# A second normalisation moved to the head of the next step in ScalarE's order, two more q tiles ahead of the attention chain, and transposed reloads spread between W_down's loads

## The chip, the cores and the metric

The kernel runs on one core of a Trainium2 chip. The metric is device microseconds of one execution. Each time below is the median of a few executions; most agree within 0.3%. The profile is one execution taken by the hardware profiler. Its span is some 2 us shorter than the time of the same execution (849.7 against 851.4 us before).

## The reference, cut to what matters

```python
# A_x: 1 x 2048 x 1024, bf16; 32 heads of 32; F = 3584
x = A_x
h  = x + attention(layernorm(x)) @ wo          # linear attention: phi(q) kv / (phi(q) z)
h2 = h + (relu(g) * u) @ W_down                # g, u = layernorm(h) @ W_gate, @ W_up
# phi(t) = where(t > 0, t + 1, exp(t)) + 1e-6
```

The kernel works on tiles of 128 tokens, 16 in all.

## The kernel before: the parts that matter

Five engines (TensorE, VectorE, ScalarE, GpSimd, and SyncE, which issues the DMAs) run their own instruction lists, each in program order, and meet through semaphores. A helper adds every operation to the list of one engine and works out the waits, so **program order in the source is the order in each engine's queue**.

The attention chain has 16 steps (`t`). `a1` makes one q tile: 8 matmuls on TensorE into a bank (a slice of its output memory), then `exp` on ScalarE, then two VectorE operations (together "phi"). `a2(t)` multiplies phi(q) by kv ("num") and divides on VectorE. `a4(t-2)` is the output projection, then the residual `h`, its statistics, and the second normalisation ("norm2"). The time from one num to the next is called the pitch.

```python
def phi(b, w, dst_ap, dst_buf, name):            # end of every a1
    PL.add("act", exp(out=Et, in_=bank(b)))      # L533
    PL.add("dve", tensor_scalar(out=E2t, Et, min 1.0, add 1e-6))          # L535
    PL.add("dve", scalar_tensor_tensor(out=dst_ap, bank(b), E2t))         # L538
# ...
def a4(st):
    # 16 matmuls into a pair of banks
    PL.add("dve", tensor_tensor(out=hsb[:, hs, :], ps pair + x2))         # L698, "h"
    dma(h_scr <- hsb)
    ks = ln_stats(hsb[:, hs, :], ...)    # dve: bn_stats x2 (L509), aggr, ve (L514); pool: rstd (L517)
    PL.add("pool", nmr = -mean * rstd)                                    # L706
    PL.add("act", xn = Identity(hsb * rstd + nmr))                        # L710, "norm2"
    # DMA of xn: transposed into hnT (tiles 0-7), or to hn_scr in DRAM (tiles 8-15)
# ...
for ct in range(NG):
    a1(0, ct)                            # q tiles of the first 512 tokens
rest = [(r, ct) for r in range(1, NSB) for ct in range(NG)]     # 24 more
LAG = 2
for t in range(NST):
    a2(t)                                # "num t"; num 4, 8, 12 need q tiles of the next 512 tokens
    if rest: a1(*rest.pop(0))            # q tile a
    if t >= LAG: a4(t - LAG)
    if rest: a1(*rest.pop(0))            # q tile b
    if t == 13: s_sums()                 # "S sums": four VectorE sums for the product stage
    if t == 14: [f_() for f_ in t_sums(0) + t_sums(1)]          # "T sums": eight more
for t in range(NST - LAG, NST):
    a4(t)
```

After the chain come two passes, each a product stage (gate and up, by Strassen products P1, P7, P6, ...) and four W_down rounds. The start of P6, the third product of the first pair, is used below as the mark of the chain's end. W_down streams through a ring of four chunks. Before the second pass eight tiles of norm2's output are reloaded with transposition.

```python
for i, (hf, dh) in enumerate(rounds):            # four W_down rounds of a pass
    if p_ + 1 < NPASS and i == 0:
        for t in range(TPP):                     # eight transposed reloads, in one burst
            dma_t(sl_ht[t], hnT[...], hn_scr[...], reads=[B_hnscr[t]], writes=[B_hnT[t]])
    d_round(p_, hf, dh, ...)                     # per chunk of W_down: 16 matmuls, then load_wd_next()
    if p_ + 1 < NPASS and i == 1:
        s_sums()
```

## Time and profile before

| what | before |
|---|---|
| time, median | 852.99 us (852.23 to 853.74) |
| span in the profile, granted TensorE clock | 849.7 us, 0.972 |
| TensorE busy | 791.0 us, 93% |
| num 0 to the first P6 product | 142.2 to 308.1 us |
| TensorE's wait in the first W_down round | 6.9 us |

From the profile page of the kernel before: the span, then busy tenths in 40 slices of 21 us for TensorE and VectorE and the granted clock, then the chain that ended last.

```profile
span 849.7 us, 9959 instructions
...
PE   8999999878685689999999969999999999999998
...
DVE  7455427746566966676667210315666766521111
...
PEclk9999999989897899999999989999999999999999
...
PE 81%; DVE 9%; issue 4%; SPq 2%; ACT 1%; POOL 1%; DMA 1%; DVEq 0%; ACTq 0%; POOLq 0%
```

TensorE has holes in two places: slices 8 to 15 (the attention chain), and slice 24 (the first W_down round). The clock falls in five of them (9, 11, 13, 14 and 24).

From the waits of the kernel before (engine, line, who was waited for: us in total, times, longest):

```profile
DVE RX L535 <- ACT RX L533: 90.1, 43, 10.9
PE ps L499 <- DVE RAB L538: 24.2, 7, 6.7
PE ps L499 <- DVE RO L674: 11.7, 11, 5.6
PE ps L499 <- DMA RW<-in_B_W_down_dram: 6.9, 1, 6.9
```

VectorE waits for `exp` (L533), and TensorE waits for phi (L538, before a num). Neither says yet why `exp` is late. The timeline does: TensorE, VectorE and ScalarE in one full step of the kernel before (start, duration, what; in brackets the idle time before and what ended it).

```profile
181.61 1.89 PE L499 MATMUL ps<-RAB,RC 128*128 128x512 bf16 x8
...
185.06 0.15 DVE L514 TENSOR_SCALAR ve<-mv 128x1 f32<-128x1 f32 x1
...
186.33 1.24 ACT L710 ACTIVATE xn<-hsb,nmr,rstd 128x1024 bf16<-128x1024 bf16 x1 [7.39 <-POOL nmr L706]
187.47 1.06 ACT L533 ACTIVATE RX<-ps 128x512 bf16<-128x512 f32 x2
...
188.08 0.29 DVE L535 TENSOR_SCALAR RX<-RX 128x512 bf16<-128x512 bf16 x1 [2.87 <-ACT RX L533]
```

The matmuls of q tile b (the first line) are done at 183.5 us, and ScalarE is idle. But norm2 stands ahead of their `exp` in ScalarE's queue. It needs the statistics that VectorE ends at 185.2 us and GpSimd's two small operations, so it starts at 186.3 and `exp` at 187.5. VectorE meanwhile idles 2.87 us: it waits for ScalarE, which waits for GpSimd, which waited for VectorE.

The first W_down round in the timeline of the kernel before, TensorE and SyncE's queue of DMA issues:

```profile
475.49 13.98 PE L499 MATMUL ps<-RW,RAB 128*128 128x512 bf16 x63
...
476.17 12.21 SPq L436 DMA_TRANSPOSE hnT<-hn_scr  x8
488.56 1.87 SPq L432 DMA_DIRECT2D RX<-h_scr  x4
490.53 2.73 SPq L432 DMA_DIRECT2D RW<-in_B_W_down_dram  x4
496.39 3.88 PE L499 MATMUL ps<-RW,RAB 128*128 128x512 bf16 x11 [6.93 <-DMA RW<-in_B_W_down_dram]
```

TensorE works through the four chunks in the ring in 14 us. The slot of the first was free at about 479, but the load that refills it is issued at 490.5, behind eight reloads and four loads of h.

### The profile page before, as it was taken

To read this page: it belongs to the slowest core of one execution; us is meant where nothing else is said; L and a number is where in the kernel's file an instruction comes from. 1 tells how busy PE (TensorE), PEld (TensorE's weight loads), DVE (VectorE), ACT (ScalarE), POOL (GpSimd) and SP (SyncE) were. 2 spreads that over 40 slices of the span, in tenths; PEclk is the share of its full clock that TensorE was granted. 3 is DMA by queue.
4 is the path that set the end of the run, shared out by engine and by line. 5 is a ranking of instruction groups with operands and counts; after the bars stand their busy time and mean duration, and the time that the engine had idled before them with its cause. 6 is when DMAs were issued, how large, how long until landed. Compare 5 with 4: busy or idle time off the path is not lost.

```text
span 849.7 us, 9959 instructions
## 1 busy us (share of the span) xinstructions
PE 791.0 (93%) x3719; PEld 362.6 (43%) x3791; DVE 433.2 (51%) x900; ACT 245.8 (29%) x402; POOL 25.2 (3%) x60
## 2 busy tenths in 40 slices
PE   8999999878685689999999969999999999999998
PEld 3444444433332234444444424444444444444443
DVE  7455427746566966676667210315666766521111
ACT  4333333122221145444554100003454445410000
POOL 2000000000000110000000000000000000000000
PEclk9999999989897899999999989999999999999999
DMA  8687200334334453331333665653233224026652
GB/s 297 174 203 194 61 2 11 78 87 100 91 108 88 121 176 100 99 94 57 99 100 95 141 202 191 211 201 117 81 100 100 75 75 123 1 75 200 206 189 98
DMA packets 160128, 102.37 MB, mean 120 GB/s; under 512 B 50384, under 2 KB 153040, under 8 KB 160080
## 3 DMA queue, kind: packets, MB, share of 16 engines
q1 hardware_dynamic: 160080, 101.73, 41.0%
q8 instruction: 30, 0.49, 0.2%
q14 instruction: 18, 0.15, 0.1%
HBM read 79.69 MB, written 10.49 MB: 106 GB/s over the span
## 4 chain that ended last, share of the span: by engine, by line
PE 81%; DVE 9%; issue 4%; SPq 2%; ACT 1%; POOL 1%; DMA 1%; DVEq 0%; ACTq 0%; POOLq 0%
PE ps L499 81%; DVE st L509 2%; DVE hsb L698 2%; DVE RO L674 1%; SPq L436 1%; ACT RX L533 1%; DVE RAB L538 1%; DVE RX L535 1%; DMA RW<-in_B_W_down_dram 1%; POOL rstd L517 1%; DVE rden L667 0%; DVE RC L728 0%; DVE dtmp L663 0%; DVE mv L512 0%; DMA RO<-RO 0%
## 5 line engine op out<-in xcount | busy, mean ns | idle before, releaser
L499 PE MATMUL ps<-RW,RAB 128*128 128x512 bf16 x878 | 194.3, 381 | 7.9 <-DMA RW<-in_B_W_down_dram 6.9
L499 PE MATMUL ps<-RC,RE 128*128 128x512 f16 x672 | 156.0, 382 | 2.8 <-ACT ps L755 2.8
L499 PEld LDWEIGHTS ps<-RW,RAB 128*128 128x128 bf16 x896 | 87.9, 98 | 113.9 <-DMA RW<-in_B_W_down_dram 7.4
L499 PE MATMUL ps<-RAB 128*128 128x512 bf16 x499 | 112.4, 379 | 1.6 <-ACT RAB L571 0.7
L755 ACT ACTIVATE ps<-ps 128x512 f32<-128x512 f32 x112 | 65.1, 582 | 161.2 <-PE ps L499 160.6
L861 DVE TENSOR_TENSOR RX<-ps,RX 128x512 bf16<-128x512 f32 x32 | 22.1, 692 | 174.4 <-PE ps L499 153.8
L499 PE MATMUL ps<-hnT,wring 128*128 128x512 bf16 x448 | 105.8, 379 | 0.0
L499 PEld LDWEIGHTS ps<-RC,RE 128*128 128x128 f16 x672 | 66.0, 98 | 83.3 <-ACT ps L755 3.3
L755 ACT ACTIVATE RO<-ps 128x512 f32<-128x512 f32 x112 | 66.7, 597 | 53.9 <-PE ps L499 53.9
L805 DVE TENSOR_TENSOR RAB<-ps,RAB 128x512 bf16<-128x512 f32 x28 | 19.4, 692 | 112.6 <-PE ps L499 112.6
L499 PEld LDWEIGHTS ps<-RAB 128*128 128x128 bf16 x512 | 49.3, 98 | 57.9 <-ACT RAB L571 0.9
L499 PEld LDWEIGHTS ps<-hnT,wring 128*128 128x128 bf16 x448 | 43.9, 98 | 53.1 <-issue 0.5
L499 PE MATMUL ps<-RW,RO 128*128 128x512 bf16 x249 | 62.4, 403 | 2.7 <-DMA RO<-RO 2.1
L535 DVE TENSOR_SCALAR RX<-RX 128x512 bf16<-128x512 bf16 x64 | 18.6, 291 | 90.3 <-ACT RX L533 90.1
L499 PE MATMUL ps<-RAB,RC 128*128 128x512 bf16 x250 | 64.2, 407 | 0.4
L533 ACT ACTIVATE RX<-ps 128x512 bf16<-128x512 f32 x64 | 37.2, 592 | 70.6 <-PE ps L499 45.8
L499 PE MATMUL ps<-RC,wring 128*128 128x512 f16 x224 | 52.9, 379 | 0.0
L710 ACT ACTIVATE xn<-hsb,nmr,rstd 128x1024 bf16<-128x1024 bf16 x16 | 19.8, 1240 | 114.1 <-POOL nmr L706 114.1
L755 ACT ACTIVATE RAB<-ps 128x512 bf16<-128x512 f32 x56 | 33.4, 597 | 62.0 <-PE ps L499 62.0
L499 PE MATMUL ps<-hnT,RE 128*128 128x512 bf16 x196 | 46.9, 379 | 1.5
L499 PE MATMUL ps<-kvz,RAB 128*128 128x132 bf16 x128 | 14.2, 230 | 36.6 <-DVE RAB L538 24.2
L744 DVE TENSOR_TENSOR RE<-wring,RE 128x512 f16<-128x512 bf16 x112 | 47.2, 421 | 1.9
(56 smaller groups left out, 537.5 us busy)
## 6 DMA issues: line engine op xcount, KB each, us to landing
RW<-in_B_W_down_dram SPq DMA_DIRECT2D x56, 512.0 KB, 3.5
wring<-in_B_W_gate_dram SPq DMA_DIRECT2D x28, 512.0 KB, 3.7
wring<-in_B_W_up_dram SPq DMA_DIRECT2D x28, 512.0 KB, 4.8
RAB<-in_A_wqkv_dram SPq DMA_DIRECT2D x8, 512.0 KB, 8.4
RX<-in_A_x_dram SPq DMA_DIRECT2D x16, 256.0 KB, 3.1
h_scr<-hsb SPq DMA_DIRECT2D x16, 256.0 KB, 3.2
RX<-h_scr SPq DMA_DIRECT2D x32, 128.0 KB, 3.6
out_dram<-RX SPq DMA_DIRECT2D x32, 128.0 KB, 1.7
```

Source lines behind the costliest of these rows:

```text
L436: return PL.add("sp", lambda e: e.dma_start_transpose(dst_ap, src_ap), reads=reads, writes=writes, slot=slot, name=name)
L499: lambda e: e.matmul(out_ap, lhsT, rhs, start=start, stop=stop, skip_group_check=skip),
L509: PL.add("dve", lambda e, c=c: e.bn_stats(out=st6[:, k, c * 6:(c + 1) * 6], in_=src_full[:, c * BCH:(c + 1) * BCH]), reads=[src_chunk_bufs ...
L517: PL.add("pool", lambda e: e.tensor_tensor(out=rstd[:, k, :], in0=ve[:, k, :], in1=neghalf[:], op=ALU.pow), reads=[B_ve[k], B_neghalf], wr ...
L533: PL.add("act", lambda e: e.activation(out=Et[:, k, 0:w], in_=src, func=ACTF.Exp), reads=[B_bank[b]], writes=[B_E[k]], name=name + "_exp")
L535: PL.add("dve", lambda e: e.tensor_scalar(out=E2t[:, k, 0:w], in0=Et[:, k, 0:w], scalar1=1.0, scalar2=1e-6, op0=ALU.min, op1=ALU.add), rea ...
L698: PL.add("dve", lambda e: e.tensor_tensor(out=hsb[:, hs, :], in0=ps[:, b:b + 2, :], in1=x2[:, xs, :].rearrange("p (a c) -> p a c", a=2), o ...
L710: PL.add("act", lambda e: e.activation(out=xn[:, kx, :], in_=hsb[:, hs, :], func=ACTF.Identity, bias=nmr[:, ks, :], scale=rstd[:, ks, :]), ...
L744: PL.add("dve", lambda e: e.tensor_tensor(out=Tring[:, k, j], in0=in0, in1=in1, op=ALU.subtract), reads=reads, writes=[B_T[k][j]], name="T ...
L755: PL.add("act", lambda e: e.activation(out=dst, in_=src, func=func), reads=reads, writes=writes, name=name)
L805: PL.add("dve", lambda e: e.tensor_tensor(out=hh[:, f1, 0:SBW], in0=bank(BA[1]), in1=r11[:, rr, :], op=ALU.mult), reads=[B_bank[BA[1]], B_ ...
L861: PL.add("dve", lambda e: e.tensor_tensor(out=outst[:, k, :], in0=bank(banks4[j], NW), in1=hres[:, k, :], op=ALU.add), reads=[B_bank[banks ...
```

## The change

Three parts. No arithmetic is added or removed.

1. Norm2 of tile t-3 moves to the head of step t, so that in ScalarE's order it no longer stands between `exp` a and `exp` b of the step that makes its input. In ScalarE's own list that is one place later, behind `exp` b, because `a2` puts nothing on ScalarE. (The T sums move from step 14 to 15.)
2. Two q tiles are made ahead of the loop, so that num 4, 8 and 12 find their last q tile a whole step old.
3. The eight reloads are spread: one after each of the first four W_down loads of rounds 0 and 1. (The second pass's S sums, which read what is reloaded, move from behind round 1 into round 2.)

```diff
+            a4_k[st] = ks
+
+        a4_k = {}
+
+        def a4_norm(st):            # norm2 and the DMA of its output, unchanged
+            hs = st % NHS
+            ks = a4_k[st]
             kx = st % NXN
@@ d_round, after each chunk
                 load_wd_next()
-                for _ in range(2):
-                    if fill:
-                        fill.pop(0)()
+                if fill:
+                    fill.pop(0)()
@@ the chain
         rest = [(r, ct) for r in range(1, NSB) for ct in range(NG)]
+        for _ in range(2):
+            a1(*rest.pop(0))
         LAG = 2
-        fill = []
-        for t in range(NST):
-            a2(t)
+        for t in range(NST + LAG + 1):
+            if t >= LAG + 1:
+                a4_norm(t - LAG - 1)
+            if t < NST:
+                a2(t)
             if rest:
                 a1(*rest.pop(0))
-            if t >= LAG:
+            if LAG <= t < NST + LAG:
                 a4(t - LAG)
 ...
-            if t == 14:
+            if t == 15:
                 for f_ in t_sums(0) + t_sums(1):
                     f_()
-        for t in range(NST - LAG, NST):
-            a4(t)
@@ the W_down rounds
-                if p_ + 1 < NPASS and i == 0:
-                    for t in range(TPP):
-                        dma_t(... "T5s_%d" % t ...)
-                d_round(p_, hf, dh, ...)
-                if p_ + 1 < NPASS and i == 1:
-                    s_sums()
+                late = []
+                if p_ + 1 < NPASS and i < 2:
+                    for t in range(i * STB, (i + 1) * STB):
+                        late.append(lambda t=t: dma_t(... "T5s_%d" % t ...))
+                if p_ + 1 < NPASS and i == 2:
+                    late.append(s_sums)
+                d_round(p_, hf, dh, ..., fill=late)
```

More of the change, by code (lines that the diff above doesn't have):

```diff
@@ L984, in bass_sequential_preLN__linear_attn_block__glu_gated_reglu__prompt_kernel @@
             for i, (hf, dh) in enumerate(rounds):
-                if p_ + 1 < NPASS and i == 0:
-                    for t in range(TPP):
-                        dma_t(sl_ht[t], hnT[:, :, t * P:(t + 1) * P], hn_scr[t * P:(t + 1) * P, :],
-                              "T5s_%d" % t, reads=[B_hnscr[t]], writes=[B_hnT[t]])
-                d_round(p_, hf, dh, [0, 1, 2, 3] if i % 2 == 0 else [4, 5, 6, 7])
-                if p_ + 1 < NPASS and i == 1:
-                    s_sums()
+                late = []
+                if p_ + 1 < NPASS and i < 2:
+                    for t in range(i * STB, (i + 1) * STB):
+                        late.append(lambda t=t: dma_t(
+                            sl_ht[t], hnT[:, :, t * P:(t + 1) * P], hn_scr[t * P:(t + 1) * P, :],
+                            "T5s_%d" % t, reads=[B_hnscr[t]], writes=[B_hnT[t]]))
+                if p_ + 1 < NPASS and i == 2:
+                    late.append(s_sums)
+                d_round(p_, hf, dh, [0, 1, 2, 3] if i % 2 == 0 else [4, 5, 6, 7], fill=late)
+                assert not late
         PL.finalize(eng_sems)
```

## The prediction

> **What bounds the kernel now.** The chain of waits is 81% TensorE. By the busy table by stage, two stretches have holes: the attention chain, from the first num tile at 142 us to the first P6 product at 308.1 us (about 42 us idle, granted clock 0.89 and 0.85), and the start of the first W_down round, 475.8 to 502 us (7 us idle, clock 0.87).
>
> *Chain.* By the timeline a full step needs on TensorE 0.48 (num) + 1.73 (q tile) + 3.45 (output projection) + 1.73 (q tile) = 7.4 us, on VectorE 2.4 (divide) + 0.94 (phi) + 2.96 (h and statistics) + 0.94 (phi) = 7.2 us. But the ten steps from num 2 (151.6) to num 12 (264.7) take 11.3 us each. The cause is ScalarE's order: exp a, norm2, exp b. Norm2 waits for VectorE's statistics and GpSimd (2.9 us from their end to VectorE's next phi), and exp b, whose matmul is done, waits behind it: VectorE idles 2.9 us, released by ScalarE, in each step. Num 4, 8 and 12 consume the last q tile at once, so TensorE waits 6.5 to 6.7 us there, then runs slow: 8 matmuls take 3.6 us instead of 1.9. The Trainium skill ("TensorE: Matmul & The Clock Gate", Part 1) states half rate after idling; 0.43 us apart against 0.22, these agree.
>
> *W_down.* Eight transposed reloads hold SyncE's queue from 476.2 to 488.4, so the fifth W_down chunk, its slot free at 479, is issued at 490.5. TensorE waits 6.9 us, then 20 matmuls take 5.8 us instead of 4.4: 8.3 us together.
>
> **The change** adds and removes no arithmetic.
> 1. Norm2 of tile t-3 heads step t in ScalarE's order. Between its statistics (step t-1) and phi a VectorE has phi b and the divide, 3.3 us, against the 2.9 us path: exp b no longer waits, exp a hardly.
> 2. Two q tiles (3.5 us TensorE) move ahead, so num 4, 8 and 12 find theirs a step old. The 1.4 us wait before num 0 goes.
> 3. Each reload follows one W_down load. A chunk lasts 3.45 us on TensorE; by the DMA shares, load plus reload need about 3 us. The stall should go.
>
> **Sum.** Num 0 moves to 145.7 us. Steps 0 and 1 (no projection) take 8.3 us; nine steps at 7.45 end at 221. VectorE, 2.4 us behind, bounds the tail: five divides 12, seven h 20.7, S and T sums 8.3, idle 1 to 2, so its last statistics end near 266.5, and P6 starts 3.1 us later, as now: 269.6 against 308.1. Saving 38.5 us. W_down: of 8.3 us I expect 8. 853.0 - 38.5 - 8.0 = 806.5; the interlock will not be perfect: **807 us**, range 800 to 817. Faster by over 2%: 0.97; within 2%: 0.025; slower: 0.005.
>
> **What would show it.** Step 1: VectorE's wait on exp (90 us in all) falls by over 25 us, step pitch 7.4 to 7.8 us. Step 2: TensorE's wait on phi (24.2 us) nearly vanishes. Step 3: no TensorE wait on W_down, and round one is 8 us shorter. VectorE bounds the tail; the 2.8 us wait before P6 stays or grows.
>
> **What would make it wrong.** If the 0.4 us slack before exp a is missing, norm2 moves its wait to exp a: pitch 8 to 9 us, 812 to 820 in total. If reloads slow W_down loads beyond 3.45 us each, part of the 8 us stays.

## The result, and the profile after

The time after is **802.23 us** (802.01 to 802.45, 2 runs) against 852.99 us; ratio 0.9405, 95% interval 0.9365 to 0.9445.

The same lines of the profile page, after:

```profile
span 800.3 us, 9969 instructions
...
PE   8999999999987799999999999999999999999998
...
DVE  7455535799999656756755103137657657401111
...
PEclk9999999999998999999999999999999999999999
...
PE 91%; DVE 5%; issue 1%; DMA 1%; ACT 1%; SPq 0%; POOL 0%; DVEq 0%; POOLq 0%; ACTq 0%
```

The holes of slices 8 to 11 and of the W_down round are gone. What is left is in slices 12 to 14, the tail of the chain. In slices 9 to 11 VectorE and TensorE are both at 90% or more.

The waits after. The line of TensorE waiting for phi (L538) and the one of TensorE waiting for W_down are not in the list any more. L762 is ScalarE's copy of a bank in the product stage. (Norm2's line is now L717.)

```profile
DVE RX L535 <- ACT RX L533: 58.6, 32, 10.9
...
PE ps L499 <- DVE RO L674: 7.4, 6, 5.5
...
PE ps L499 <- ACT ps L762: 4.8, 1, 4.8
```

A full step after (timeline of TensorE, VectorE and ScalarE):

```profile
181.63 1.89 PE L499 MATMUL ps<-RAB,RC 128*128 128x512 bf16 x8
...
183.61 0.60 ACT L533 ACTIVATE RX<-ps 128x512 bf16<-128x512 f32 x1 [3.28 <-PE ps L499]
...
184.71 0.15 DVE L514 TENSOR_SCALAR ve<-mv 128x1 f32<-128x1 f32 x1
184.78 0.28 DVE L535 TENSOR_SCALAR RX<-RX 128x512 bf16<-128x512 bf16 x1
...
185.97 1.24 ACT L717 ACTIVATE xn<-hsb,nmr,rstd 128x1024 bf16<-128x1024 bf16 x1 [1.76 <-DVE dtmp L663]
...
187.12 0.57 ACT L533 ACTIVATE RX<-ps 128x512 bf16<-128x512 f32 x1
...
188.09 0.28 DVE L535 TENSOR_SCALAR RX<-RX 128x512 bf16<-128x512 bf16 x1
```

`exp` b starts as soon as its matmuls are done, and VectorE goes from the statistics to phi b with no gap, where it lost 2.87 us before. Norm2 still has to wait for its input, which GpSimd ends at 185.85 us, and `exp` a (187.12) still stands behind it, 1.4 us after its own matmuls. But VectorE has the divide to do first and takes up phi a at 188.09, 0.4 us after that `exp` has ended: the wait has moved to where nobody is kept by it. From num 2 (153.61 us) to num 11 (220.22) a step takes 7.40 us. The first P6 product starts at 267.1 us instead of 308.1: 41.0 us of the 49.4 by which the span fell. The other 8.4 us come after it.

The first W_down round after (timeline of TensorE and SyncE's queue):

```profile
434.55 29.73 PE L499 MATMUL ps<-RW,RAB 128*128 128x512 bf16 x134
...
438.25 0.38 SPq L432 DMA_DIRECT2D RW<-in_B_W_down_dram  x1
438.68 1.45 SPq L436 DMA_TRANSPOSE hnT<-hn_scr  x1
441.70 0.39 SPq L432 DMA_DIRECT2D RW<-in_B_W_down_dram  x1
442.13 1.24 SPq L436 DMA_TRANSPOSE hnT<-hn_scr  x1
```

Each refill now goes out 3.5 us after the one before, as its slot comes free, and TensorE runs through without a wait.

### The profile page after: what moved, and what is told of

Its sections match the earlier page's. It is cut to its first block, busy times and chain, and to the rows that moved or that the text cites. A ratio compares the mean times of both kernels' runs of the same rounds, so it can differ in the third digit from the quotient of the medians.

```text
span 800.3 us, 9969 instructions
## 1 busy us (share of the span) xinstructions
PE 777.7 (97%) x3719; PEld 360.3 (45%) x3791; DVE 432.3 (54%) x900; ACT 246.8 (31%) x402; POOL 25.2 (3%) x60
## 4 chain that ended last, share of the span: by engine, by line
PE 91%; DVE 5%; issue 1%; DMA 1%; ACT 1%; SPq 0%; POOL 0%; DVEq 0%; POOLq 0%; ACTq 0%
PE ps L499 91%; DVE st L509 1%; DVE hsb L698 1%; DVE RO L674 1%; DMA RAB<-in_A_wqkv_dram 1%; ACT RX L533 1%; DVE RAB L538 1%; DVE RC L735 0%; DVE RX L535 0%; DVE RE L751 0%; DVE rden L667 0%; DVE dtmp L663 0%; SPq L432 0%; DVE mv L512 0%; PE ps L568 0%
## 5 line engine op out<-in xcount | busy, mean ns | idle before, releaser
L762 ACT ACTIVATE ps<-ps 128x512 f32<-128x512 f32 x112 | 65.1, 582 | 152.9 <-PE ps L499 149.1
L762 ACT ACTIVATE RO<-ps 128x512 f32<-128x512 f32 x112 | 66.7, 597 | 53.7 <-PE ps L499 53.7
L499 PE MATMUL ps<-RW,RO 128*128 128x512 bf16 x249 | 59.1, 388 | 0.4
L499 PE MATMUL ps<-RAB,RC 128*128 128x512 bf16 x250 | 58.0, 379 | 0.3
L762 ACT ACTIVATE RAB<-ps 128x512 bf16<-128x512 f32 x56 | 33.4, 597 | 62.2 <-PE ps L499 62.2
L535 DVE TENSOR_SCALAR RX<-RX 128x512 bf16<-128x512 bf16 x64 | 18.4, 288 | 58.6 <-ACT RX L533 58.6
L751 DVE TENSOR_TENSOR RE<-wring 128x512 f16<-128x512 bf16 x112 | 42.0, 416 | 0.0
L819 DVE TENSOR_TENSOR RO<-ps,RO 128x512 f32<-128x512 f32 x56 | 38.7, 691 | 5.5 <-ACT RO L762 5.4
```

Source lines behind the costliest of these rows:

```text
L499: lambda e: e.matmul(out_ap, lhsT, rhs, start=start, stop=stop, skip_group_check=skip),
L535: PL.add("dve", lambda e: e.tensor_scalar(out=E2t[:, k, 0:w], in0=Et[:, k, 0:w], scalar1=1.0, scalar2=1e-6, op0=ALU.min, op1=ALU.add), rea ...
L751: PL.add("dve", lambda e: e.tensor_tensor(out=Tring[:, k, j], in0=in0, in1=in1, op=ALU.subtract), reads=reads, writes=[B_T[k][j]], name="T ...
L762: PL.add("act", lambda e: e.activation(out=dst, in_=src, func=func), reads=reads, writes=writes, name=name)
L819: PL.add("dve", lambda e, w=w: e.tensor_tensor(out=ftmp[:, 4 + w, :], in0=bank(BF_[w]), in1=ftmp[:, 2 + w, :], op=ALU.add), reads=[B_bank[ ...
```

## The experiments

Twelve kernels, all correct, each timed against the kernel before in three rounds on the same chip. "Before" was 851.09, 851.52 and 850.66 us in the three groups. The first four runs of the table were on one chip and the other eight on another, so differences of under 1 us between groups say nothing. P6 is the start of the first P6 product in the profile, that is, the end of the chain.

| run | time, us | ratio to before | P6 at, us |
|---|---|---|---|
| norm_only | 818.03 | 0.9611 | 274.0 |
| q_only | 834.78 | 0.9813 | 292.6 |
| reload_only | 841.26 | 0.9889 | 307.9 |
| norm_and_q | 810.16 | 0.9520 | 267.5 |
| norm_mid | 802.13 | 0.9423 | 267.5 |
| half_bursts | 805.51 | 0.9467 | 268.0 |
| q_one | 801.41 | 0.9419 | 266.5 |
| q_six | 833.81 | 0.9798 | 289.7 |
| t_early | 798.29 | 0.9384 | 264.8 |
| s_late | 799.06 | 0.9392 | 263.3 |
| norms_late | 795.20 | 0.9346 | 262.5 |
| tail | 790.05 | 0.9285 | 256.9 |

By the record's rule for 2%, q_only and q_six are "unclear" and reload_only is "same". Their 95% intervals (0.9794 to 0.9831, 0.9779 to 0.9818, 0.9870 to 0.9908) all stay below 1: these gains are real, but near or under 2%.

### The parts one at a time

**norm_only**: the change without its second and third part.

```diff
-        for _ in range(2):            # against the changed kernel
-            a1(*rest.pop(0))
   and the reloads in one burst, as in the kernel before
```

> Only the second normalisation moves (no extra q tiles, reloads in one burst as before). Theory: it removes the 2.9 us that VectorE loses in every step, so the pitch falls from 10.1 to about 7.4 us, but num 4, 8 and 12 still consume a q tile made one step earlier. VectorE runs 2.4 us behind, its phi b ends about 9.65 us after its step began, so TensorE should wait about 2 to 2.5 us at num 4, 8 and 12 (6.7 us before). Time about 818 us (815 to 823), W_down stall unchanged at about 7 us. Rival: the stall at every fourth num is the true cause and the normalisation only a follower; then the waits at num 4, 8 and 12 stay near 6 us and the time stays above 830.

Measured: 818.03 us (816.87 to 819.15). TensorE's waits, norm_only:

```profile
PE ps L499 <- DVE RAB L538: 7.5, 4, 2.2
```

The four waits are 1.4 us at num 0 and 1.9, 2.0 and 2.2 us at num 4, 8 and 12 (2 to 2.5 were expected), where there were 6.5 to 6.7 us. The rival falls: most of the stall at every fourth num was itself made by norm2 in ScalarE's queue.

**q_only**: the kernel before with the second part alone.

```diff
         rest = [(r, ct) for r in range(1, NSB) for ct in range(NG)]
+        for _ in range(2):
+            a1(*rest.pop(0))
```

> Only the two extra q tiles ahead (norm2 between the two exps as before). Theory: waits on phi at num 4, 8, 12 vanish (24 us of waits before), but VectorE still loses 2.9 us per step to exp b behind norm2, pitch 10.1 us throughout, so num 12 comes near 250 us instead of 264.7; time about 836 us (833 to 841). Rival: the slack of one step hides norm2's wait as well, pitch near 7.4 us, time near 811. Second rival: neither part alone helps, time above 845.

Measured: 834.78 us. TensorE no longer waits for phi, but for the divide (L674):

```profile
PE ps L499 <- DVE RO L674: 19.7, 19, 5.6
```

Num 5 to num 11 follow each other in 10.1 to 10.2 us (177.97 to 239.01 us in the trace for six steps). The slack of a step doesn't hide norm2's wait. Nor does more of it:

**q_six**: the same with six tiles ahead.

```diff
+        for _ in range(6):
+            a1(*rest.pop(0))
```

> The kernel before with six q tiles ahead instead of none (norm2 in its old place, reloads in one burst). Theory: with norm2 in its old place VectorE loses 2.9 us in every step that has a q tile after norm2, however far ahead the tiles are; each pair moved ahead costs 3.5 us in front and turns one step of 10.1 us into one of 5.35 us, 1.3 us gained per pair: 834.8 - 2.6 = 832 us (830 to 834). Rival: more slack hides norm2's wait, the pitch falls towards 7.4 us, time below 820.

Measured: 833.81 us (832.38 to 835.45), within the expected range, its median 1.8 us above the 832 worked out; P6 comes 2.9 us sooner than in q_only, but the wait for W_down was 7.6 us in this profile and 6.2 in that of q_only. The pitch from num 5 to num 10 is 10.1 to 10.2 us again. The wait is a loop through three engines' queues, and work done ahead of a loop does not shorten it.

**q_one**: the changed kernel with one tile ahead instead of two.

```diff
-        for _ in range(2):
+        for _ in range(1):
             a1(*rest.pop(0))
```

> The changed kernel with one q tile ahead instead of two. Theory: with one tile ahead the last tile that num 4, 8 or 12 needs is the first q tile of the step before, whose phi ends 5.8 us after that step began, before the num at 7.4 us: no wait, so the second tile buys nothing; 801.5 us (800.5 to 803). Rival: two are needed, waits of 1 us or more at each fourth num, 804 to 806 us.

Measured: 801.41 us, and no wait for phi. One tile is enough; the second buys nothing that these runs can see.

**reload_only** and **norm_and_q**: the third part alone, and everything but it.

```diff
   reload_only = the kernel before, with the "late" list of the change in the W_down rounds
   norm_and_q  = the changed kernel, with the burst of eight reloads of the kernel before
```

> Only the reloads spread, one after each of the first four W_down loads of rounds 0 and 1. Theory: the stall of 6.9 us and the slow matmuls after it vanish, nothing else moves: 844.6 us (843.5 to 845.5). Rival: what the reloads cost is DMA time, not the place in the queue, so W_down loads now come late by a little in several chunks: TensorE waits on W_down stay at 3 us or more, time above 847.

> Everything but the spread of the reloads. Theory: the parts at different places in the program add up: 802.2 + 8.4 = 810.6 us (809.5 to 812), with the W_down stall back at 6.9 us and the chain as in the changed kernel (first P6 product at 267 us). Rival: the spread also changed the chain or the chain's earlier end changes the stall: off by 2 us or more.

Measured: 841.26 and 810.16 us. In reload_only the wait on W_down is gone. Its gain of 9.8 us is above the expected 8.4, so 841.26 us misses the expected range on the fast side. In the two profiles 8.4 us are gained from the start of the first W_down round on. The rest lies at P6, long before a reload is issued: the first eight P6 matmuls took 1.90 us here and 3.50 in the profile of the kernel before, after the same wait of 2.77 us. The clock came out differently. (No trace shows P6 in the other executions.) This is the line in the timeline of the kernel before:

```profile
308.12 3.50 PE L499 MATMUL ps<-RC,RE 128*128 128x512 f16 x8 [2.77 <-ACT ps L755]
```

and in that of reload_only:

```profile
307.86 1.90 PE L499 MATMUL ps<-RC,RE 128*128 128x512 f16 x8 [2.77 <-ACT ps L755]
```

The gains of the three runs (33.1, 16.3 and 9.8 us) add up to 59.2, and the whole change gained 50.8. Norm2 and the q tiles overlap: together 40.9 us, not 49.4, because both take from the stall at every fourth num. After norm_only the q tiles are worth 7.9 us, about its 7.5 us of waits for phi. The reloads stand apart: norm_and_q less the changed kernel (timed in other rounds) is 7.9 us. The wait for W_down in the profile of norm_and_q was 5.4 us, not the 6.9 that were expected.

### Is it norm2's place, or the age of its input?

**norm_mid**: norm2 goes back between the two exps, but for the tile one step older.

```diff
-            if t >= LAG + 1:
-                a4_norm(t - LAG - 1)
             if t < NST:
                 a2(t)
             if rest:
                 a1(*rest.pop(0))
+            if t >= LAG + 1:
+                a4_norm(t - LAG - 1)
```

> The changed kernel with norm2 put back between the two exps of a step, but for the tile one step older (the tile that the changed kernel normalises at the head of the same step). Theory: what counts is that norm2's input is ready when ScalarE reaches it, not its place between the exps; with an input one step old exp b never waits, so the time is that of the changed kernel, 802 us (800.5 to 803.5), pitch 7.4 us. Rival: the place itself costs, because exp b then always stands behind a 1.2 us activation; the pitch rises by up to 1 us and the time to 808 or more.

Measured: 802.13 us. ScalarE's timeline, norm_mid:

```profile
193.35 0.60 ACT L533 ACTIVATE RX<-ps 128x512 bf16<-128x512 f32 x1 [1.58 <-PE ps L499]
193.85 1.23 ACT L717 ACTIVATE xn<-hsb,nmr,rstd 128x1024 bf16<-128x1024 bf16 x1
198.54 0.60 ACT L533 ACTIVATE RX<-ps 128x512 bf16<-128x512 f32 x1 [3.47 <-PE ps L499]
```

Norm2 now starts straight behind `exp` a, with its input long there, and the `exp` after it waits only for its matmuls. So in this loop it is the age of the input that counts, not the place between the two exps. An instruction of 1.2 us costs nothing there as long as what it waits for is there when its turn comes and the engine has time for it (ScalarE idles 3.47 us before the next `exp`).

### Is it the reloads' DMA time, or the length of the burst?

**half_bursts**: the changed kernel with its reloads in bursts of four ahead of rounds 0 and 1.

```diff
+                if p_ + 1 < NPASS and i < 2:
+                    while late:
+                        late.pop(0)()
                 d_round(p_, hf, dh, ..., fill=late)
```

> The changed kernel with its reloads in two bursts of four, ahead of rounds 0 and 1, instead of one after each W_down load. Theory: the four chunks that are already loaded last 13.8 us; a burst of eight (12.2 us of queue, 2 us of h loads, then 5.8 us to landing) overruns that by 6.9, a burst of four (6.1 us of queue) ends with the load landing about 14 to 15 us after the round's start: a stall of 0 to 1.5 us in each of the two rounds and no slow matmuls; 803 us (802 to 805). Rival: the reloads' time is simply added to the round they stand ahead of, so two halves cost as much as one whole: two stalls of 4 us, 810 us.

Measured: 805.51 us, half a microsecond above the expected range. TensorE's timeline, half_bursts:

```profile
435.77 13.98 PE L499 MATMUL ps<-RW,RAB 128*128 128x512 bf16 x64
451.40 24.35 PE L499 MATMUL ps<-RW,RAB 128*128 128x512 bf16 x112 [1.65 <-DMA RW<-in_B_W_down_dram]
477.61 7.73 PE L499 MATMUL ps<-RW,RAB 128*128 128x512 bf16 x35 [1.86 <-DMA RW<-in_B_W_down_dram]
```

Two waits of 1.65 and 1.86 us, with no slow matmuls after them; I had said 0 to 1.5. The refill was issued 9.6 us after the round began (6.8 us of reloads, 1.9 us of h loads) and landed 6.0 us later, against 13.8 us of work in the ring. The rival, that reload time simply adds up to 8 us however it is divided, falls: two half bursts cost 3.5 us of waiting, one whole burst 6.9 and the slow matmuls after it. The ring absorbs a late refill up to its length, and the overrun is what is paid. But DMA time has a share in the overrun. The first refill took 5.9 us to land behind the burst of eight and 6.0 behind that of four; in the first round of the changed kernel refills take 3.8 to 4.7. At that, the one here would have come 13.4 to 14.3 us after the round began, and at most 0.5 of the wait of 1.65 us would be left; of the 6.9 us some 1 to 2 would go (estimates from these numbers). In the five profiles with the whole burst this landing took 4.3, 4.9, 5.1, 5.9 and 6.5 us, and TensorE waited 5.4, 6.2, 6.8, 6.9 and 7.6. So the burst does harm twice: it holds the queue, and the refill behind it lands later. Whether the reloads still in flight slow it, or the three refills issued right behind it, is not shown.

### The tail, and a version that beats both

After the change VectorE bounds the chain's last steps. The timeline shows num 15 waiting 5.5 us for the divide of step 14, which stands behind the S sums in VectorE's queue, and P6 waiting 4.8 us for ScalarE, which has norm2 of tiles 14 and 15 to do first (at 262.2 and 265.3 us; the expectation below names tile 13 too, but its norm2 is over at 257.6, before the wait begins). These tiles belong to the second pass, and nothing in the first needs them. Four runs test that, each built on the changed kernel.

**t_early**: the eight T sums go into VectorE's gaps among the first q tiles.

```diff
+        early = t_sums(0) + t_sums(1)
         for ct in range(NG):
             a1(0, ct)
+            early.pop(0)()
 ...
-            if t == 15:
-                for f_ in t_sums(0) + t_sums(1):
-                    f_()
```

> The changed kernel with the eight T sums of the first product pair (3.0 us of VectorE) moved from the tail to the first eight q tiles, where VectorE waits 0.71 us per tile for exp. Theory: VectorE bounds the tail, so the last statistics end earlier, but only until TensorE's last projection bounds them: about 2.3 us sooner, 800 us (799 to 801.5). Rival: TensorE or ScalarE bounds the tail, nothing moves: 802.2.

Measured: 798.29 us, P6 at 264.83 us, so 2.3 us sooner as expected. The time fell by more (3.9 us) and misses the range by 0.7 us on the fast side, as the first P6 matmuls ran fast here (1.90 us for eight) and slow in the changed kernel (3.42).

**s_late**: t_early, with the S sums behind step 15.

```diff
-            if t == 13:
+            if t == 15:
                 s_sums()
```

> t_early with the S sums after step 15 in VectorE's order, norm2 where the changed kernel has it. Theory: num 15 no longer waits 5.6 us and TensorE is done with the projections 5 us sooner, but P6 still waits on ScalarE for norm2 of tile 15, which follows VectorE's last statistics, and VectorE's work is the same: P6 near 263.6 us, 797 us (796 to 798.5), hardly better than t_early (798.3); TensorE's wait on ScalarE grows to about 6.5 us. Rival: the place of the S sums is what won the 8 us of the run called tail: 792 us or less.

**norms_late**: t_early, with the last two norm2 behind the first product pair.

```diff
-        for t in range(NST + LAG + 1):
-            if t >= LAG + 1:
+        for t in range(NST + LAG):
+            if LAG + 1 <= t < NST + 1:
                 a4_norm(t - LAG - 1)
 ...
             strassen_pair(p_, q, fill)
+            if p_ == 0 and q == 0:
+                a4_norm(NST - 2)
+                a4_norm(NST - 1)
```

> t_early with the last two norm2 after the first product pair, S sums after step 13 as in the changed kernel. Theory: P6 is then bounded by TensorE's last projection and the banks of the last h: P6 near 262 us, 795.5 us (794 to 797); the wait of num 15 behind the S sums (5.6 us) stays. With s_late that makes the two edits worth more together (790) than the sum of each alone. Rival: the norms' place alone won the 8 us: 792 us or less.

**tail**: both.

> As t_early, and the S sums stand after step 15 in VectorE's order instead of step 13, and the last two norm2 come after the first product pair in ScalarE's order. Theory: num 15 no longer waits 5.6 us behind the S sums and P6 no longer waits 4.8 us for norm2 of tiles 13 to 15, but only for the banks of the last two h: first P6 product near 258 us instead of 267.1, time about 793.5 us (791 to 797). Rival: VectorE's work in the tail is the same in amount, so P6 still comes when its queue is done: 799 us or more.

Measured: s_late 799.06 us, norms_late 795.20, tail **790.05** us (789.80 to 790.77). TensorE's line for P6 in s_late:

```profile
263.25 3.60 PE L499 MATMUL ps<-RC,RE 128*128 128x512 f16 x8 [6.60 <-ACT ps L762]
```

Here the wait for ScalarE grew from 2.77 us (t_early) to 6.60, as expected: TensorE is done earlier and waits longer at the next place. P6 starts 1.6 us sooner than in t_early, yet the run is 0.8 us slower and misses its range by half a microsecond. The eight matmuls ran slowly again, 3.60 us, and that took the gain. In tail neither wait is left, and its time lies a microsecond below its expected range. All of TensorE's waits in tail (the last two lie at the start of the kernel):

```profile
PE ps L499 <- DVE RO L674: 2.6, 7, 0.5
PE ps L499 <- DMA RO<-RO: 1.5, 1, 1.5
PE ps L499 <- POOL hsb L394: 1.4, 1, 1.4
PE ps L499 <- ACT RAB L571: 0.7, 1, 0.7
```

Over t_early the two edits give -0.8 and +3.1 us alone, and +8.2 us together. Each removes one of two waits in series, and alone it leaves, or lengthens, the other. The granted clock in the profile of tail is 1.0.

## Why the prediction was right, point by point

| term | predicted | measured |
|---|---|---|
| num 0 starts | 145.7 us | 145.76 |
| num 2 starts | 154.0 | 153.61 |
| pitch of steps 2 to 10 | 7.45 us | 7.40 |
| VectorE behind TensorE at step 11 | 2.4 us | 2.42 |
| VectorE's step 11 to its last statistics | 43.1 us | 41.4 |
| from there to P6 | 3.1 us | 3.1 |
| P6 | 269.6 us | 267.1 |
| saved in the W_down round | 8 of 8.3 us | 8.4 (the span after P6) |
| time | 807 us (800 to 817) | 802.2 |

- *"exp b, whose matmul is done, waits behind it."* Shown. The Trainium skill ("TensorE: Matmul & The Clock Gate", Part 1, the note on engine queue depths) says that ScalarE and VectorE take instructions strictly first in, first out. These traces agree: in the kernel before, `exp` b sat from 183.5 to 187.5 us, with ScalarE idle until 186.3. norm_mid shows that with an input one step old, norm2's place in the queue is free.
- *"exp b no longer waits, exp a hardly"*, by a margin of 0.4 us. Right for VectorE: no wait of VectorE for ScalarE is left in steps 2 to 10, and that wait fell from 90.1 to 58.6 us in total, above the 25 us named. `exp` a itself does wait behind norm2 (1.4 us in the step shown), and the margin of 0.4 us is what is left of the slack.
- *"Num 4, 8 and 12 find theirs a step old."* Right, and more than was needed: q_one gives the same time.
- *"Each reload follows one W_down load ... The stall should go."* Right. half_bursts shows that the damage came from the burst outlasting the ring, by its hold on the queue and by the slower landing of the refill behind it.
- *The tail.* VectorE bounds it, as said, and the wait before P6 grew from 2.8 to 4.8 us. This is where the sum was mis-sized: I gave VectorE 1 to 2 us of idle time over the tail and rounded up; the timeline shows 0.53 us of waiting for TensorE. That is 1.7 of the 2.5 us by which P6 came sooner than predicted.

Of the 4.8 us between 807 and 802.2, 2.5 lie before P6 and 0.4 in the W_down round. Another 0.5 is an allowance for an imperfect interlock, which was not needed: TensorE was 99% busy from 152 to 221 us (68.4 of 68.9 us). And the median time fell 1.4 us more than the spans of the two profiles did, which is the spread of the runs.

One part was luck. The sum leaves out the clock at P6. The matmuls after the longer wait ran slowly (3.42 us for eight), but so they did in the profile before (3.50), and the two cancel. Of the five profiles with a wait of 2.77 us before P6 it is the only slow one; against a fast one the saving would have been some 1.6 us smaller (an estimate, 3.50 less 1.90).

What stays open: why the clock, after the same wait of 2.77 us, was at full rate in four profiles and low in one. After a wait of 4.5 us or more before P6 it was low in all seven. The runs show that it is so, not what decides it. It moves P6's next microseconds by 1.6.

## What to carry to other kernels

In an engine that takes its queue in order, ask of each instruction whether its input is there when its turn comes. If it isn't, everything behind it waits too; that is harmless only while nobody needs what stands behind it, as with `exp` a after the change. When the input comes back from the engine that is kept waiting, the loss repeats in every step and no slack elsewhere hides it. What a burst on a DMA queue cost here is the time by which the load behind it came after its ring ran dry (even four reloads were too many), and spread reloads cost no wait at all, so interleave them with the loads. Where two waits follow one another, removing one alone can show little or nothing: look for what TensorE will wait for next before calling an edit useless.

## What the Trainium skill lacked or had wrong

- "TensorE: Matmul & The Clock Gate", Part 1, puts the low clock after about 3.4 us of idle time and says that the window runs freely. In these runs shorter waits were followed by it too: one of 1.62 us (q_only, num 5, with another of 0.24 right after) by eight matmuls in 3.42 us instead of 1.89, at a mean granted clock of 0.53 over 3.3 us, and one of 1.99 us (norm_only, num 8) by eight in 2.88 us, at 0.65 over 2.7 us. The length alone doesn't decide: 1.93 and 2.17 us (num 4 and 12 of norm_only) and 1.62 us (num 7 of reload_only) had no slow matmuls after them, and waits of 2.77 us went both ways (3.50 and 1.90 us for eight). The same part does tell, of another kernel, that frequent very short idle times make the clock swing, but gives no length for them. For planning, a wait of 1.6 us may already cost another 1.5.
- "DMA: Bandwidth & Descriptors", Issuing engines are not separate DMA queues, calls the sequencer's issue time usually small relative to the DMA. For transposed reloads it was not: at the median 1.31 us of SyncE's queue for each in the burst of eight, against 3.9 us to landing and 0.37 to 0.39 us of queue for a plain 512 KB load in the changed kernel. Eight of them, with four small loads, held back a W_down load by 11.5 us.
- No page that I consulted gives a rule for how long a burst a prefetch ring can absorb. Here 13.8 us of work in the ring was overrun by 6.9 us with eight reloads ahead of the refill, and by 1.65 us with four.
